# A three-stage kernel (pooled attention, eight-expert MoE, max-of-three FFN): paired k/v transposes, a second products point per iteration, and the first group's columns in six pieces

## The chip, the cores and the metric

One core of one Trainium2 chip runs the whole program. The metric is device microseconds for one launch; lower is better. Engines are named as in the profile: PE (TensorE matmul), PEld (its weight load), DVE (VectorE), ACT (ScalarE), POOL (GpSimd), SP (the queue that issues most DMAs).

## What is computed

Cut to what matters:

```python
# 1. attention, q/k/v [8, 8, 576, 64]; k and v are mean-pooled by 8 along the sequence (576 -> 72)
scores = q @ k_pooled.T / sqrt(64);  attn = softmax(scores);  x = attn @ v_pooled      # -> [4608, 512]
# 2. MoE with 8 experts, top 1 of cosine logits / tau; w1 [8,512,1024], w2 [8,1024,512]
out[token] = gate[token] * (relu(x[token] @ w1[e]) @ w2[e])
# 3. FFN, m1..m3 [512, 768], mo [768, 512]
y = max(x @ m1, x @ m2, x @ m3) @ mo                                                     # [4608, 512]
```

Everything is float32. Matmuls of stages 2 and 3 split each operand into a high and a low float32r part and take three products.

## The kernel before, in words

**Stage 1 (attention, about the first 205 us).** There are 36 tiles of 128 query rows; batches b = 0..7 are taken in pairs, nine tiles a pair, the middle tile being half of one batch and half of the next. A Python loop (line 1441) writes one software-pipelined iteration `it` after the other into the engines' queues: `boundary()`, then `stage_s` of tile it-1 (scores, line 380), `stage_a` of tile it-3 (transposes of the softmaxed scores, line 427), `stage_q` of tile it (transposes of q, line 365), `stage_e` (exp), `stage_x` of tile it-4 (attention times v, line 447), then the jobs that `todo[it]` names. Each engine executes its queue in this order.

Jobs are steps of `prep_steps(b)` (line 248): the pooling of k and v by adding halves three times (`pool_k2`, line 263, and `pool_v`, line 275, both on POOL, for b > 1; `pool_k`, line 255, a DVE reduction, for b = 0 and 1), `dup_k` (line 271, ACT copies pooled k beside itself so that a transpose gives k on both halves of the partitions), `spread_v` (line 280, POOL writes v by head into `vbd`), `trans_k` (line 291: five PE transposes, ACT copies into the block-diagonal `kbd`), `trans_v` (line 303: five more transposes of pooled v and a copy into `vT`), and `vdot` (line 313: ten small matmuls of `vT` with the normalized expert embedding, which give the router's logits in extra columns of `vbd`). k is cut in rows 128, 128, 128, 120, 72 (`KC`) and v in 128 x 4, 64 (`RC`). With `need` the iteration at which batch b is first used, the steps for b > 1 are due at need-7 (-5 for b = 2), need-3 (-2 for b = 2), need-1, need, need, need+1, need+2 (lines 1428 to 1434).

**Routing (inside stage 1 and the start of stage 2).** Chains of small DVE steps (`rank_steps` line 565, `early_steps` line 668, `final_steps`) are dripped in by `fill(n)` between the operations of the iterations (line 875). When a chain yields "pe" it wants the PE: `boundary()` (line 890) turns the state "pe" into "products" at one call, at the next call it runs the step that issues the matmuls (whose state is then "wait"), and at the call after that it lets the chain go on with the results. `boundary()` is called once an iteration. After the first 24 tiles the chain rank_steps(2) + early_steps is queued (at it 27, where `dense[0]` becomes 2); its end, `early_start` (line 924), loads the first expert's weights and issues the gather of the first item's rows (`gather`, line 953, an indirect DMA on POOL into `xrow`).

**Stage 2 (MoE, about 205 to 726 us).** `run` (line 1291) takes 22 items: 18 pairs of 128-row blocks and then singles. An item has eight steps: four weight pieces of w1 (`mm1`) and four of w2 (`mm2`). Each step splits the piece two steps ahead (`split`: ACT casts `whi`, then DVE or POOL subtracts for `wlo`), and `hhi`, `hlo` are ACT and DVE results that the next product needs. `between` (line 1320) is called twice a step. Once the routing is done it advances two generators: `conversions` (cv) and `combinations` (cb), which prepare the weights of stage 3. In the last pair and the singles (from item 17 on, `last_pairs`) `between` advances cb twice instead of once. The end of cb is `columns(0, 1)` (line 1236): it loads the first 768 columns of stage 2's result in four pieces of [128, 2, 2, 192] through one buffer `yr` (two DMAs a piece on SP), waits three yields, and then makes the sums and splits that stage 3 needs (`sums`, line 1260: six DVE and three ACT instructions in five yields).

**Stage 3 (FFN, from 726 us).** `second` (line 1530) takes six groups of 768 rows; the columns of each later group are loaded whole, in two pieces with two buffers, while the group before it finishes.

Of the kernel before, what the change touches and what calls it, by code (L numbers as in the profile page):

```python
# [8 lines left out]
F32 = mybir.dt.float32  # L9
# [5 lines left out]
A = mybir.AluOpType  # L15
# [6 lines left out]
def attention_moe_moe_kernel(  # L22
# [93 lines left out]
    if True:  # L116
# [61 lines left out]
        if True:  # L178
# [69 lines left out]
            def prep_steps(b):  # L248
                kt, vt = kv[b]
                kb, vb = kbds[b % 3], vbds[b % 3]  # L250
                kp = qp.tile([P, 5, 2, D], F32, tag="kp", name=f"kp{b}")
                vp = qp.tile([P, 5, D], F32, tag="vp", name=f"vp{b}")
                vT = qp.tile([D, 5, P], F32, tag="vT", name=f"vT{b}", bufs=1)

                def pool_k(c):
# [5 lines left out]
                        pool_k(c)  # L261

                def pool_k2():
                    for c0, c1, n in ((0, 3, P), (3, 4, KC[3]), (4, 5, KC[4])):
                        for w in (4, 2, 1):
                            dst = kt[0:n, c0:c1, 0:w, :] if w > 1 else kp[0:n, c0:c1, 0:1, :]
                            nc.gpsimd.tensor_tensor(
                                dst, kt[0:n, c0:c1, 0:w, :], kt[0:n, c0:c1, w : 2 * w, :], op=A.add
                            )
# [4 lines left out]

                def pool_v(c0, c1, n):
                    for w in (4, 2, 1):
                        dst = vt[0:n, c0:c1, 0:w, :] if w > 1 else vp[0:n, c0:c1, :].unsqueeze(2)
                        nc.gpsimd.tensor_tensor(dst, vt[0:n, c0:c1, 0:w, :], vt[0:n, c0:c1, w : 2 * w, :], op=A.add)

                def spread_v():  # L280
                    for c, (h0, h1) in enumerate(HS):
# [9 lines left out]
                def trans_k(cs, h0, h1):  # L291
                    ps = pq.tile([P, 512], F32, tag="pq", name=f"ptk{b}_{h0}")
                    col = 0
                    for c in cs:
                        n = KC[c]
                        nc.tensor.transpose(
                            ps[:, col : col + n], kp[0:n, c].rearrange("p two d -> p (two d)"), ident[0:n, 0:n]
                        )
                        col += n
                    nc.scalar.copy(kb[0:D, h0:h1, 0, :], ps[0:D, 0:col].rearrange("p (h s) -> p h s", s=SP))  # L300
                    nc.scalar.copy(kb[D:P, h0:h1, 1, :], ps[D:P, 0:col].rearrange("p (h s) -> p h s", s=SP))

                def trans_v(c0, c1):
                    ps = pq.tile([P, 512], F32, tag="pq", name=f"ptv{b}_{c0}")
# [31 lines left out]
                        lambda: vdot(),  # L336
                    ]
                if b == 1:
                    pk = [lambda: (pool_k(0), pool_k(1)), lambda: (pool_k(2), pool_k(3)), lambda: pool_k(4)]
                    pk += [lambda: (pool_v(0, 4, P), pool_v(4, 5, 64))]  # L340
                else:
                    pk = [lambda: (pool_k2(), pool_v(0, 4, P), pool_v(4, 5, 64))]
                return pk + [
                    lambda: (dup_k(), spread_v()),
                    lambda: trans_k(range(4), 0, 7),
# [832 lines left out]
            def combinations():  # L1178

                for i in range(3):
                    while i not in whole:
                        yield
                    m_ = mraw[i]
                    for p_ in range(F2C // 2):
                        fa, fb = slice(p_ * P, (p_ + 1) * P), slice((3 + p_) * P, (4 + p_) * P)
                        a11, a12, a21, a22 = m_[:, 0:2, fa], m_[:, 2:4, fa], m_[:, 0:2, fb], m_[:, 2:4, fb]  # L1190
                        st = tl["stage"].tile([P, 2, 14, P], F32R, tag="wst", name=f"wst{i}_{p_}")
                        hi, lo = st[:, 0], st[:, 1]
                        sm = tl["stage"].tile([P, 8, P], F32, tag="wsum", name=f"wsum{i}_{p_}")
# [12 lines left out]
                        nc.scalar.copy(hi[:, 6:14, :], sm)  # L1206
                        gt_(lo[:, 4:6, :], a22, hi[:, 4:6, :].bitcast(F32), op=A.subtract)
                        yield
                        gt_(lo[:, 6:14, :], sm, hi[:, 6:14, :].bitcast(F32), op=A.subtract)
                        nc.gpsimd.dma_start(wdram[3 * p_ + i], st.rearrange("p a b f -> p (a b f)").bitcast(F32))  # L1210
                        if p_ == F2C // 2 - 1:
                            combined.append(i)
                        for _ in range(10):
                            yield
                while 3 not in whole:
                    yield
                for f in range(F2C):
# [10 lines left out]
                for _ in columns(0, 1):  # L1228
                    yield

            yhl = []
# [1 line left out]
            def split_o(f):  # L1233
                nc.vector.tensor_tensor(olo[:, f, :], mraw[3][:, f, :], ohi[:, f, :].bitcast(F32), op=A.subtract)

            def columns(g, bufs):

                w_ = HW // 2 if bufs == 1 else HW
                rows = []
                for c in range(2):
                    for n in range(0, HW, w_):
                        t = tl["yr"].tile([P, 2, 2, w_], F32, tag="yr", name=f"yr{g}_{c}_{n}", bufs=bufs)
# [3 lines left out]
                        if bufs == 1:  # L1250
                            for _ in range(3):
                                yield
                            yield from sums(t, c, n, w_)
                        rows.append((t, c, n, w_))
                if bufs > 1:
                    yield
                    for a_ in rows:
                        yield from sums(*a_)

            def sums(t, c, n, w_):  # L1260
                hi, lo = (x_[:, :, n : n + w_] for x_ in yhl[2 * c : 2 * c + 2])
# [58 lines left out]
            def between(half, p_=0):  # L1320

                if not routed:
                    return
                if queue:
                    if half == 0:
                        boundary(p_ in (0, 1, 2, 3, 7))
                    fill(3)
                else:
                    for _ in range(1 + (half and p_ % 2)):
                        next(cv, None)  # L1330
                    next(cb, None)
                    if last_pairs:
                        next(cb, None)

            p0 = prep_steps(0)
            p0[0]()
# [91 lines left out]
            for b in range(1, B):  # L1428
                need = (b // 2) * 9 + (0 if b % 2 == 0 else 4)
                at_ = [need - 7, need - 3, need - 1, need, need, need + 1, need + 2]  # L1430
                at_ = {1: [2, 3, 3, 2, 3, 4, 4, 5, 6, 7], 2: [need - 5, need - 2] + at_[2:]}.get(b, at_)
                for j, t in enumerate(at_):
                    todo.setdefault(t, []).append((b, j))
            qorder = [(m, p_) for m in range(B // 2) for p_ in range(3)]
# [6 lines left out]
            for it in range(NT + 4):  # L1441
# [14 lines left out]
                    load_q(*qorder[qnext])  # L1456
                    qnext += 1
                while kvnext < B and kvnext * 4.5 - 11 <= it:
                    kv[kvnext] = (load_rows("kraw", k, kvnext, KC), load_rows("vraw", v, kvnext, RC))
                    kvnext += 1  # L1460
                if 0 <= it - 1 < NT:
                    stage_s(it - 1)
# [7 lines left out]
                    squares.pop()()  # L1470
                if it >= NT + 2:
                    next(first)
                if 0 <= it - 4 < NT:
                    stage_x(it - 4)
                if it == NT + 1:
# [54 lines left out]
    def second(st, groups, again=False):  # L1530
# [140 lines left out]
        for k_ in range(3):  # L1671
            load_chunk(k_)
        tokens(groups[0])
        ahead = columns(groups[0], 2) if again else iter(())
        for g in groups:
            for _ in ahead:
                pass
            for n in range(CH):
                quad(g, n, groups.index(g) * CH + n)
            nxt = g + 1 in groups  # L1680
            ahead = columns(g + 1, 2) if nxt else iter(())
            next(ahead, None)
            if nxt:
                tokens(g + 1)
# [80 lines left out]
```

## Time and profile before

| what | value |
|---|---|
| median of the runs, lowest, highest | 1281.93 us, 1281.42, 1282.61 |
| the profiled execution's own time | 1281.78 us |
| its span (first to last instruction) | 1279.9 us |
| PE busy | 1225.6 us of the span |

The 1.9 us between the span and the time of the profiled execution lie around the program. A row of a timeline is: start us, duration us, engine, line, operation, tiles written <- read, shape, count, and in brackets how long the engine sat idle just before it and what ended that. A row of the waits is: who waited for whom: us in total, times, the longest. A row of windows is: the stretch, its length, busy us of each engine with the number of instructions, the granted share of the PE's full clock, the mean busy share of the DMA engines, GB/s.

### The profile page before, as it was taken

What the parts mean: (1) busy time and instruction counts of PE and PEld (TensorE: products, weight loads), DVE (VectorE), ACT (ScalarE), POOL (GpSimd) and SP (SyncE); (2) the same over time, 40 slices, a digit from 0 to 9 for tenths busy, and PEclk for the clock granted to TensorE, in tenths of its full rate; (3) what the DMA queues carried; (4) which work ended last, traced back from release to release, by engine and by line L of the source; (5) the groups of instructions that cost most, each with busy time, mean ns of one, the idle gap of its engine ahead of it and who ended that gap; (6) DMA issues with size and microseconds to landing.
All of it is one profiled execution on the core that took longest, in us unless ns stands there. A gap on an engine that the chain in (4) does not pass through costs nothing. (4 is left out here: it accounts for less than half of the span.)

```text
span 1279.9 us, 22372 instructions
## 1 busy us (share of the span) xinstructions
PE 1225.6 (96%) x8281; PEld 1164.2 (91%) x8281; DVE 802.7 (63%) x1551; ACT 581.4 (45%) x1040; POOL 346.5 (27%) x357
## 2 busy tenths in 40 slices
PE   4999998989899999999989999999999999999997
PEld 3888787989899999999979899899998998998995
DVE  6776784788789899899654446355256345345450
ACT  2566555435566666666535423333234223223231
POOL 7985643434500403223000300201302103103101
PEclk9899999999999999999999999999999999999999
DMA  9867335421885644953516768367376475664631
GB/s 261 252 202 214 121 113 206 150 82 35 232 286 199 217 147 161 292 175 132 190 50 229 265 238 304 115 248 280 119 266 231 165 253 209 210 240 181 226 146 52
DMA packets 100088, 246.21 MB, mean 192 GB/s; under 512 B 17102, under 2 KB 57084, under 8 KB 91908
## 3 DMA queue, kind: packets, MB, share of 16 engines
q1 hardware_dynamic: 90660, 201.67, 47.3%
q0 software_dynamic: 9312, 43.04, 9.5%
q8 instruction: 67, 1.10, 0.3%
q14 instruction: 49, 0.40, 0.1%
HBM read 252.23 MB, written 46.98 MB: 234 GB/s over the span
## 5 line engine op out<-in xcount | busy, mean ns | idle before, releaser
L1579 PE MATMUL p<-yhi,wt 128*128 128x384 f32 x1512 | 387.2, 336 | 0.7 <-ACT yo L1093 0.7
L1579 PEld LDWEIGHTS p<-yhi,wt 128*128 128x128 f32 x1512 | 273.5, 188 | 1.4 <-ACT yo L1093 0.9
L1579 PE MATMUL p<-ylo,wt 128*128 128x384 f32 x756 | 254.0, 336 | 0.0
L1587 ACT COPY s<-p 128x384 f32<-128x384 f32 x162 | 77.8, 480 | 222.2 <-PE p L1579 214.0
L1021 PE MATMUL ph<-xhi,whi 128*128 128x256 f32 x576 | 164.9, 286 | 8.0 <-DVE hlo L1037 8.0
L1069 PE MATMUL py<-hhi,wlo 128*128 128x256 f32 x576 | 164.0, 285 | 3.3 <-DVE wlo L1001 3.3
L1069 PE MATMUL py<-hhi,whi 128*128 128x256 f32 x576 | 165.4, 287 | 1.0 <-ACT whi L999 1.0
L1021 PE MATMUL ph<-xhi,wlo 128*128 128x256 f32 x576 | 163.8, 284 | 1.9 <-DVE wlo L1001 1.9
L1021 PE MATMUL ph<-xlo,whi 128*128 128x256 f32 x576 | 163.7, 284 | 1.2 <-DVE xlo L988 1.2
L1069 PE MATMUL py<-hlo,whi 128*128 128x256 f32 x576 | 163.5, 284 | 0.0
L1579 PEld LDWEIGHTS p<-ylo,wt 128*128 128x128 f32 x756 | 142.1, 188 | 0.5
L1608 DVE TENSOR_TENSOR blk<-p,s 128x384 f32<-128x384 f32 x108 | 59.7, 553 | 114.1 <-PE p L1579 113.9
L1564 POOL DMA_INDIRECT gt<-gbuf,ix x26 | 37.1, 1428 | 322.4 <-DMA ix<-idbuf 316.0
L1021 PEld LDWEIGHTS ph<-xhi,whi 128*128 128x128 f32 x576 | 111.0, 193 | 9.6 <-DVE hlo L1037 9.2
L1069 PEld LDWEIGHTS py<-hhi,wlo 128*128 128x128 f32 x576 | 111.0, 193 | 4.1 <-DVE wlo L1001 4.1
L1021 PEld LDWEIGHTS ph<-xhi,wlo 128*128 128x128 f32 x576 | 111.2, 193 | 2.3 <-DVE wlo L1001 2.3
L1021 PEld LDWEIGHTS ph<-xlo,whi 128*128 128x128 f32 x576 | 111.1, 193 | 1.4 <-DVE xlo L988 1.4
L1069 PEld LDWEIGHTS py<-hhi,whi 128*128 128x128 f32 x576 | 111.1, 193 | 1.2 <-ACT whi L999 1.2
L1069 PEld LDWEIGHTS py<-hlo,whi 128*128 128x128 f32 x576 | 111.2, 193 | 0.0
L1001 DVE TENSOR_TENSOR wlo<-w2raw,whi 128x1024 fp32r<-128x1024 f32 x78 | 94.8, 1221 | 9.5 <-ACT whi L999 9.5
L961 POOL DMA_INDIRECT xrow<-xbuf,idg x40 | 69.6, 1740 | 113.4 <-PE px L982 87.8
L999 ACT CAST whi<-w2raw 128x1024 fp32r<-128x1024 f32 x88 | 91.8, 1044 | 5.5 <-PE py L1069 3.9
(307 smaller groups left out, 2338.0 us busy)
## 6 DMA issues: line engine op xcount, KB each, us to landing
wt<-wdram SPq DMA_DIRECT2D x51, 1792.0 KB
w1raw<-in_moe_w_dram SPq DMA_DIRECT2D x88, 512.0 KB
w2raw<-in_moe_w_dram SPq DMA_DIRECT2D x88, 512.0 KB
wdram<-wst POOLq DMA_DIRECT2D x9, 1792.0 KB, 7.2
ybuf<-yo SPq DMA_DIRECT2D x40, 256.0 KB
cvraw<-in_moe_w_dram SPq DMA_DIRECT2D x36, 256.0 KB
vraw<-in_v_dram SPq DMA_DIRECT2D x8, 1024.0 KB
xbuf<-x SPq DMA_DIRECT2D x16, 512.0 KB
```

Of the source, the lines that this page charges most:

```text
L961: nc.gpsimd.indirect_dma_start(out=t[:, j, :], out_offset=None, in_=xbuf[0:nr, :], in_offset=bass.IndirectOffsetOnAxis(ap=idg[:, b_ : b_ + ...
L999: nc.scalar.copy(hi, src)
L1001: eng.tensor_tensor(lo, src, hi.bitcast(F32), op=A.subtract)
L1021: nc.tensor.matmul(ps[:, f, :], a_[:, c, fs], b_[:, c, :], start=(n == 0), stop=(n == 3 * DC - 1))
L1069: nc.tensor.matmul(py[:, c // 2, (c % 2) * 256 : (c % 2 + 1) * 256], a_[:, f, c * P : (c + 1) * P], b_[:, f, :], start=(piece == 0 and f = ...
L1564: nc.gpsimd.indirect_dma_start(out=gt[g][:, j : j + 1], out_offset=None, in_=gbuf[:, :], in_offset=bass.IndirectOffsetOnAxis(ap=cols[j], a ...
L1579: nc.tensor.matmul(ps, a_, b_, start=(start and c + n == 0), stop=(c == 1 and n == 2), skip_group_check=True)
L1587: nc.scalar.copy(t, ps)
L1608: tt(src, add[0], add[1], op=A.add)
```

## The change

Four things.

1. **Side-by-side transposes, b > 1.** Pooled v is written beside pooled k in one tile, both in rows 128 x 4, 64. One set of five transposes gives k on the upper and v on the lower partitions of the same PSUM tile. `dup_k` and `trans_v` go; `trans_kv` copies k to both halves of `kbd` and v to `vT`. There are five steps instead of seven, and `vdot` comes one iteration earlier. `pool_k2` has two groups of rows instead of three. The first addition of `pool_v` is cut in two instructions (for all b). k is loaded by two DMAs instead of three.
2. **b = 1:** the five DVE reductions `pool_k` come at iterations 1, 2, 2, 3, 3 instead of 2, 2, 3, 3, 3.
3. **Products twice an iteration:** while `dense[0]` is 2 and it < 36, `boundary()` is called a second time, ahead of `stage_x`.
4. **Columns of the first group:** six pieces of [128, 2, 2, 128] with two buffers, the first two loaded eight yields ahead, each later one loaded when the piece two before it is done; and cb is no longer advanced twice in the last items. The later groups keep their two whole pieces.

```diff
-                vp = qp.tile([P, 5, D], F32, tag="vp", name=f"vp{b}")
+                vp = kp[:, :, 1, :] if b > 1 else qp.tile([P, 5, D], F32, tag="vp", name=f"vp{b}")
...
-                    for c0, c1, n in ((0, 3, P), (3, 4, KC[3]), (4, 5, KC[4])):
+                    for c0, c1, n in ((0, 4, P), (4, 5, RC[4])):
...
                 def pool_v(c0, c1, n):
                     for w in (4, 2, 1):
-                        dst = vt[0:n, c0:c1, 0:w, :] if w > 1 else vp[0:n, c0:c1, :].unsqueeze(2)
-                        nc.gpsimd.tensor_tensor(dst, vt[0:n, c0:c1, 0:w, :], vt[0:n, c0:c1, w : 2 * w, :], op=A.add)
+                        for a0 in range(c0, c1, 2) if w == 4 else (c0,):
+                            a1 = min(a0 + 2, c1) if w == 4 else c1
...
+                def trans_kv(cs, r0):
+                    ps = pq.tile([P, 512], F32, tag="pq", name=f"ptk{b}_{r0}")
+                    col = 0
+                    for c in cs:
+                        n = RC[c]
+                        nc.tensor.transpose(
+                            ps[:, col : col + n], kp[0:n, c].rearrange("p two d -> p (two d)"), ident[0:n, 0:n]
+                        )
+                        col += n
+                    a0 = 0
+                    while a0 < col:
...
+                        nc.scalar.copy(kb[0:D, at_[0], 0, at_[1]], src)
+                        nc.scalar.copy(kb[D:P, at_[0], 1, at_[1]], src)
+                        a0 = a1
+                    nc.scalar.copy(vT.rearrange("p c r -> p (c r)")[:, r0 : r0 + col], ps[D:P, 0:col])
...
-                    pk = [lambda: (pool_k(0), pool_k(1)), lambda: (pool_k(2), pool_k(3)), lambda: pool_k(4)]
+                    pk = [lambda c=c: pool_k(c) for c in range(5)]
...
-                    pk = [lambda: (pool_k2(), pool_v(0, 4, P), pool_v(4, 5, 64))]
+                    return [
+                        lambda: (pool_k2(), pool_v(0, 4, P), pool_v(4, 5, 64)),
+                        spread_v,
+                        lambda: trans_kv(range(4), 0),
+                        lambda: trans_kv([4], 4 * P),
+                        vdot,
+                    ]
...
-            def columns(g, bufs):
-                w_ = HW // 2 if bufs == 1 else HW
+            def columns(g, whole_=True):
+                w_ = HW if whole_ else HW // 3
...
+                load(0)
+                load(1)
+                for _ in range(1 if whole_ else 8):
                     yield
-                    for a_ in rows:
-                        yield from sums(*a_)
+                for k_ in range(len(at_)):
+                    yield from sums(*rows[k_])
+                    load(k_ + 2)
...
                     next(cb, None)
-                    if last_pairs:
-                        next(cb, None)
...
-                at_ = {1: [2, 3, 3, 2, 3, 4, 4, 5, 6, 7], 2: [need - 5, need - 2] + at_[2:]}.get(b, at_)
+                at_ = {1: [1, 2, 2, 3, 3, 2, 3, 4, 4, 5, 6, 7], 2: [need - 5, need - 2] + at_[2:4] + at_[5:6]}.get(b, at_[:4] + at_[5:6])
...
+                if dense[0] == 2 and it < NT:
+                    boundary()
```

## Rows read from the trace of the kernel before

**Rows 1.** The page: the busy time of each engine over the span.
```profile
PE 1225.6 (96%) x8281; PEld 1164.2 (91%) x8281; DVE 802.7 (63%) x1551; ACT 581.4 (45%) x1040; POOL 346.5 (27%) x357
```

**Rows 2.** Waits of PE in the first 430 us.
```profile
PE psc L401 <- DVE sh L419: 4.9, 2, 2.7
...
PE pav L455 <- DVE dt L480: 2.9, 2, 2.5
```

**Rows 3.** Windows: stage 2, its end, and a stretch of stage 1.
```profile
490.00:610.00 120.00, 120.00 (x1007) 120.00 (x1006) 109.56 (x199) 79.46 (x117) 32.54 (x17) 1.00 0.59 198
610.00:672.00 62.00, 54.88 (x430) 53.11 (x430) 36.18 (x51) 29.50 (x44) 2.00 (x2) 0.97 0.38 123
110.00:120.00 10.00, 10.00 (x78) 9.17 (x77) 7.27 (x20) 7.48 (x22) 9.65 (x15) 1.00 0.59 183
```

**Rows 4.** Timeline of PE around one batch's transposes of v.
```profile
113.12 0.24 PE L307 MATMUL ptv<-ident,vp 64*64 64x64 f32 x1
113.29 1.25 PE L401 MATMUL psc<-kbd,qT 128*128 128x144 f32 x8
...
117.29 0.63 PE L307 MATMUL ptv<-ident,vp 128*64 128x128 f32 x4
117.75 1.15 PE L401 MATMUL psc<-kbd,qT 128*128 128x144 f32 x8
```

**Rows 5.** Timeline of DVE: two points of the early routing chain.
```profile
176.48 0.15 DVE L512 TENSOR_TENSOR cnt<-cnt,prk 128x8 f32<-128x8 f32 x1
...
199.57 0.16 DVE L518 TENSOR_SCALAR idg<-va 128x10 int32<-128x10 f32 x1
```

**Rows 6.** Timeline of PE where stage 2 begins.
```profile
201.01 2.00 PE L455 MATMUL pav<-vbd,aT 128*128 128x146 f32 x12
206.34 0.33 PE L982 MATMUL px<-ident,xrow 128*128 128x128 f32 x1 [3.33 <-DMA xrow<-xbuf,idg]
...
212.02 0.38 PE L1021 MATMUL ph<-xhi,whi 128*128 128x256 f32 x1
```

**Rows 7.** Windows: the same stretch.
```profile
203.00:212.00 9.00, 5.27 (x26) 4.68 (x25) 2.85 (x7) 5.51 (x13) 6.23 (x4) 0.81 0.68 216
```

**Rows 8.** Waits of DVE from 605 to 672 us.
```profile
DVE ysum L1266 <- DMA yr<-ybuf: 10.2, 4, 2.8
```

**Rows 9.** Timeline of ACT: the last copy of items 14 to 17 of stage 2.
```profile
589.48 1.07 ACT L1080 COPY yo<-py 128x512 f32<-128x512 f32 x2 [1.90 <-PE py L1069]
...
613.38 1.07 ACT L1080 COPY yo<-py 128x512 f32<-128x512 f32 x2 [1.95 <-PE py L1069]
...
639.17 1.07 ACT L1080 COPY yo<-py 128x512 f32<-128x512 f32 x2 [1.38 <-PE py L1069]
...
671.59 1.07 ACT L1080 COPY yo<-py 128x512 f32<-128x512 f32 x2 [5.33 <-PE py L1069]
```

**Rows 10.** Timelines of SP, DVE and PE: one column piece and the product behind it.
```profile
640.08 0.89 SPq L1249 DMA_DIRECT2D yr<-ybuf  x2
...
643.34 0.56 DVE L1266 TENSOR_TENSOR ysum<-yr 128x384 f32<-128x384 f32 x1 [2.35 <-DMA yr<-ybuf]
...
648.76 0.39 PE L1021 MATMUL ph<-xhi,whi 128*128 128x256 f32 x1 [3.08 <-DVE hlo L1037]
```

**Rows 11.** Groups on POOL in stage 1, by shape: busy us, mean ns.
```profile
L278 POOL TENSOR_TENSOR vraw<-vraw 128x1024 f32<-128x1024 f32 x8 | 18.9, 2357 | 7.0 <-DMA vraw<-in_v_dram 7.0
...
L267 POOL TENSOR_TENSOR kraw<-kraw 128x768 f32<-128x768 f32 x6 | 10.8, 1808 | 0.0
L278 POOL TENSOR_TENSOR vraw<-vraw 128x512 f32<-128x512 f32 x8 | 10.2, 1272 | 0.6
```

**Rows 12.** Timelines of DVE and POOL near 32 us.
```profile
31.76 4.09 DVE L516 TENSOR_SCALAR thr<-iof 128x36 f32<-128x36 f32 x1
...
32.01 2.05 POOL L284 TENSOR_TENSOR vbd<-vp,mslot 128x128 f32<-128x128 f32 x5
34.02 2.88 POOL L267 TENSOR_TENSOR kraw<-kraw 128x768 f32<-128x768 f32 x2
```

More of the change, by code (lines that the diff above doesn't have):

```diff
@@ L276, in pool_v @@
                     for w in (4, 2, 1):
-                        dst = vt[0:n, c0:c1, 0:w, :] if w > 1 else vp[0:n, c0:c1, :].unsqueeze(2)
-                        nc.gpsimd.tensor_tensor(dst, vt[0:n, c0:c1, 0:w, :], vt[0:n, c0:c1, w : 2 * w, :], op=A.add)
+                        for a0 in range(c0, c1, 2) if w == 4 else (c0,):
+                            a1 = min(a0 + 2, c1) if w == 4 else c1
+                            dst = vt[0:n, a0:a1, 0:w, :] if w > 1 else vp[0:n, a0:a1, :].unsqueeze(2)
+                            nc.gpsimd.tensor_tensor(
+                                dst, vt[0:n, a0:a1, 0:w, :], vt[0:n, a0:a1, w : 2 * w, :], op=A.add
+                            )
                 def spread_v():
@@ L301, in trans_k @@
                     nc.scalar.copy(kb[D:P, h0:h1, 1, :], ps[D:P, 0:col].rearrange("p (h s) -> p h s", s=SP))
+                def trans_kv(cs, r0):
[5 more added lines that the diff above has]
+                            ps[:, col : col + n], kp[0:n, c].rearrange("p two d -> p (two d)"), ident[0:n, 0:n]
+                        )
+                        col += n
+                    a0 = 0
+                    while a0 < col:
+                        h, s_ = divmod(r0 + a0, SP)
+                        if s_ == 0 and col - a0 >= SP:
+                            nh = (col - a0) // SP
+                            a1 = a0 + nh * SP
+                            src, at_ = ps[0:D, a0:a1].rearrange("p (h s) -> p h s", s=SP), (slice(h, h + nh), slice(0, SP))
+                        else:
+                            a1 = min(col, a0 + SP - s_)
+                            src, at_ = ps[0:D, a0:a1], (h, slice(s_, s_ + a1 - a0))
+                        nc.scalar.copy(kb[0:D, at_[0], 0, at_[1]], src)
+                        nc.scalar.copy(kb[D:P, at_[0], 1, at_[1]], src)
+                        a0 = a1
+                    nc.scalar.copy(vT.rearrange("p c r -> p (c r)")[:, r0 : r0 + col], ps[D:P, 0:col])
                 def trans_v(c0, c1):
@@ L1227, in combinations @@
                 tl["yr"] = pool(left, "yrow0", 1, "right")
-                for _ in columns(0, 1):
+                for _ in columns(0, False):
                     yield
@@ L1234, in split_o, with load @@
                 nc.vector.tensor_tensor(olo[:, f, :], mraw[3][:, f, :], ohi[:, f, :].bitcast(F32), op=A.subtract)
-            def columns(g, bufs):
-                w_ = HW // 2 if bufs == 1 else HW
+            def columns(g, whole_=True):
+                w_ = HW if whole_ else HW // 3
+                at_ = [(c, n) for c in range(2) for n in range(0, HW, w_)]
                 rows = []
-                for c in range(2):
-                    for n in range(0, HW, w_):
-                        t = tl["yr"].tile([P, 2, 2, w_], F32, tag="yr", name=f"yr{g}_{c}_{n}", bufs=bufs)
+                def load(k_):
+                    if k_ < len(at_):
+                        c, n = at_[k_]
+                        t = tl["yr"].tile([P, 2, 2, w_], F32, tag="yr", name=f"yr{g}_{c}_{n}", bufs=2)
                         src = ybuf[:, GW * g : GW * g + GW].rearrange("(i c p) (j n) -> c p i j n", i=2, c=2, j=2)
@@ L1249, in columns @@
                             nc.sync.dma_start(t[:, i], src[c, :, i, :, n : n + w_])
[L1250 to L1253, printed above, removed]
                         rows.append((t, c, n, w_))
-                if bufs > 1:
+                load(0)
+                load(1)
+                for _ in range(1 if whole_ else 8):
                     yield
-                    for a_ in rows:
-                        yield from sums(*a_)
+                for k_ in range(len(at_)):
+                    yield from sums(*rows[k_])
+                    load(k_ + 2)
             def sums(t, c, n, w_):
@@ L1458, in attention_moe_moe_kernel @@
                 while kvnext < B and kvnext * 4.5 - 11 <= it:
-                    kv[kvnext] = (load_rows("kraw", k, kvnext, KC), load_rows("vraw", v, kvnext, RC))
+                    kv[kvnext] = (load_rows("kraw", k, kvnext, KC if kvnext < 2 else RC), load_rows("vraw", v, kvnext, RC))
                     kvnext += 1
@@ L1673, in second @@
         tokens(groups[0])
-        ahead = columns(groups[0], 2) if again else iter(())
+        ahead = columns(groups[0]) if again else iter(())
         for g in groups:
@@ L1680, in second @@
             nxt = g + 1 in groups
-            ahead = columns(g + 1, 2) if nxt else iter(())
+            ahead = columns(g + 1) if nxt else iter(())
             next(ahead, None)
```

## The prediction

> **What bounds the kernel now.** I read the page first: PE is busy for 1225.6 of 1279.9 us [rows 1], so a change can gain only by taking work from PE, by filling its 54 us of idle time, or by keeping its clock up. The windows of 10 us over the whole span then show where PE is below 10.00. In stage 2 from 490 to 610 us it is never idle at a granted clock of 1.00, with DVE at 109.56 of 120 us; from 610 to 672 us it is idle for 62 - 54.88 = 7.1 us at a mean clock of 0.97 [rows 3]. Where stage 2 begins it is idle for 3.7 of 9.0 us at a clock of 0.81 [rows 7]. In stage 1 after its first 45 us PE is full but for a few waits on DVE, the longest 2.5 and 2.7 us [rows 2]; a usual stretch has PE at 10.00, ACT at 7.48 and DVE at 7.27 of 10 us [rows 3]. Stage 3 is full of PE work and the change leaves its code as it was. So each part below is weighed by what it does to PE.
>
> **Transposes of v.** In the timeline of PE the start of each instruction follows the one before it closely, so its cost is the distance of the starts. For one batch the 64-row transpose takes 113.29 - 113.12 = 0.17 us and the four others 117.75 - 117.29 = 0.46 us [rows 4]; no PE wait stands between. The six batches b > 1 lose these five transposes each: 6 x 0.63 = **3.8 us** of PE, in a stretch where PE is the bound. The transposes of k stay five (64 rows in place of 72, 128 in place of 120). ACT's copies become eight a batch in place of nine (three of `dup_k`, four of k, two of v, against four of k, two slivers of eight columns and two of v), more of them in one iteration; ACT stands at 7.48 of 10 us [rows 3] and PE needs `kbd` an iteration later, so I cost that at nothing; without that cover it would be an ACT copy or two ahead of a score product. `vdot` one iteration earlier waits for nothing new: it moves with the v transposes. POOL's pooling must now be done by need-1 for v too; the POOL timeline has each batch pooled two iterations or more ahead of that. SP issues one DMA less a batch. Nothing queues behind these.
>
> **Products twice an iteration.** The routing chain takes from its first products' results at 176.48 to its last result `idg` at 199.57 us [rows 5], over four iterations of some 4.9 us with a wait of three `boundary()` calls in them. Written out by the calls, each of the two products is consumed one iteration earlier: the second results come two iterations, or some 9.7 us, earlier. With them go the loads of the first expert's w1 on SP and the gather on POOL. PE now stands from 203.01 (201.01 + 2.00) to 206.34 us for the gathered rows, 3.33 us [rows 6]. That wait goes even if only one iteration is won (4.9 > 3.33). The stretch 203 to 212 us also has a granted clock of 0.81, that is, part of it at 1.2 GHz: 0.19 x 9 = 1.7 us, and 9.00 - 5.27 = 3.7 us idle [rows 7]. Sum **5.4 us**. Next after the gather would be `wlo` of the first piece, which POOL makes behind ACT's cast; the weights come earlier by the same step and the cast with them. The second call's matmuls are the same ones, put before `stage_x`; PE would wait there only if POOL's slot rows were late, and those are ready an iteration ahead. Bounds: nothing (if the gather's place is taken by the weights) to 5.4; I take 5.4 since every instruction on the way moves.
>
> **Columns of the first group.** With one buffer a piece is loaded only after the piece before it is done, and used three yields later: the load issued at 640.08 us lands at 643.34, and DVE and ACT, which run in order, stand still for it [rows 10]. DVE lost 10.2 us in four such waits [rows 8]; PE's largest gap there, 3.08 us, is a wait for `hlo`, which stood behind them [rows 10]. Priced twice: by the windows, 7.1 us idle and 0.03 x 62 = 1.9 us of clock, 9.0 us [rows 3]; by the items, 671.59 - 613.38 = 58.2 us for two items where the one before them took 613.38 - 589.48 = 23.9, so 10.4 us [rows 9]. With two buffers a load is out for five yields, two and a half steps of 3 us, 7.5 us against a landing after 3.3. What is added: twelve more DVE instructions in all (six pieces of six for four), at most 12 x 0.56 = 6.7 us by the 128 x 384 one [rows 10], spread over two items in which DVE has 62 - 36.18 = 26 us free [rows 3]. I take **9.0 us**; the lower end is 4, if the hand-offs between ACT and DVE inside `sums` were behind half of it, the upper 10.4. The later groups run the same instructions in the same order: nothing.
>
> **POOL's additions and b = 1.** Small DVE operations on SBUF stall while POOL works: `thr`, 128 x 36, took 4.09 us and ended only when POOL had passed five instructions of `vbd` and the first addition of `kraw` [rows 12]. The change makes that first addition of k longer (four row groups in place of three: 2.36 in place of 1.81 us, by the same shape of v) and cuts v's 2.36 us in two of 1.27, 2.54 together [rows 11]. Since DVE did not get in between the five independent instructions of `vbd`, I expect it not to get in between two halves either. That gives longer stalls by 0.2 to 0.55 us where one falls on PE's path, three times at most as now: +0.2 to +1.6. The DVE reduction moved to it 1 falls where DVE idles for the first scores, and takes 1 us from in front of b = 1's `kbd`: -1.0 to 0. Together I take +0.4, bounds -1.5 and +1.6.
> The Trainium skill (SBUF — State Buffer, "Who interferes with whom") says the pair of ports that DVE and GpSimd share is locked for one whole instruction, and that whoever issues first holds it. By that a cut instruction would let DVE in half-way; the five instructions that `thr` sat through here speak against it.
>
> **Sum.** 1281.8 (the profiled execution; the median of the runs is 0.15 us above it) - 3.8 - 5.4 - 9.0 + 0.4 = **1264.0 us**.
>
> **Rivals.**
> - *The column stage keeps half its loss.* If DVE and ACT waiting for each other, not the load, is what PE feels, 4 to 5 us are won in place of 9. For it: with conversions the same kind of hand-off runs at full PE, which speaks against. 1268.5.
> - *The earlier chain does not reach the gather.* A step that ends in "pe" an iteration later than I count, or POOL slot rows that come late, leaves the wait at 203 us: 1264.0 + 5.4 = 1269.4. Against it is the margin of two iterations.
> - *DVE gets in between the halves.* Each stall that meets v's first addition is then shorter by 1.1 us, on the three PE waits of this kind up to 3.3 us [rows 2, 11]: 1261. For it speaks only that these are separate instructions.
> - *Slower: POOL's longer first addition catches DVE in more places.* The place is the routing steps of stage 1, dripped between operations on which PE waits. One hit costs PE up to 2.5 us [rows 2] and, if the clock falls as at 203 us, 1.7 us more [rows 7], so 4.2. One new hit for each of the six batches would be 25 us: 1264.0 + 25.2 = 1289. It decides from five new hits (21 us against 18 won). For it: POOL is at 9.65 of 10 us beside the pooling [rows 3]; against it: its total work falls, and today only three of the many overlaps cost PE anything.
>
> **How the numbers follow.** The forecast as summed, within 3 us, has 0.60; half the columns 0.15; the gather unmoved 0.06; DVE let in 0.10; slower 0.03; and 0.06 for two of the misses at once, about 1273, or for a gain that is nearly all given back. About 0.2%, 2.6 us, is what a measurement of this kernel can tell from no change. All cases but the slower one and a piece of the last lie far below that bound: faster 0.95, same 0.02, slower 0.03. The range takes in the forecast's bounds (9.0 to 10.4 in the columns, -1.5 in the last term: 1260.7), DVE let in, half the columns and the gather unmoved: 1259.5 to 1270.5; what is left out is 1273 and above and a thin lower edge.
>
> **What would show it.** Right: no `ptv` rows, and five transposes a batch less on PE; `idg` near 190 us and no PE wait for `xrow`; the clock at 1.00 near 205 us; no wait of DVE or ACT on `yr` between 600 and 672 us, and items 16 and 17 of stage 2 at 24 us each. Wrong: gaps of PE behind `hlo` in those items though the loads are in; DVE operations of 4 us or more in stage 1 in more places than now, with PE idle behind `sh` or `dt`; a granted clock below 1.00 in new stretches of stage 1.

## The result, and the profile after

The changed kernel takes 1268.39 us (median of 4 runs, 1264.20 to 1270.12) against 1282.27 us (4 runs, 1281.42 to 1282.78). The ratio is 0.9887, with a 95% interval of [0.9869, 0.9906]: faster by 12.1 to 16.8 us. The forecast was 1264.0 us, within 1259.5 to 1270.5. The profiled execution took 1268.24 us, 13.5 us less than the one before, with a span of 1266.5 us. In the page PE has 8281 - 8251 = 30 instructions less, the five transposes of six batches:

```profile
PE 1223.4 (97%) x8251; PEld 1165.0 (92%) x8251; DVE 805.8 (64%) x1563; ACT 579.8 (46%) x1040; POOL 344.7 (27%) x347
```

**Where the time went.** Six stretches and the items 6 to 15, which take 239.0 us in every run and are left out, add up to the whole span. Their bounds are starts in the timelines: `pqT` of tile 9 and of tile 35 on PE, and the last `yo` copy of items 0, 5, 15 and 17 of stage 2 on ACT. In us, one profiled execution each; the kernels further down are the experiments of the next section (the last one is the ninth).

| kernel | to tile 9 | tiles 9 to 35 | to item 0 | items 1 to 5 | items 16, 17 | rest | span |
|---|---|---|---|---|---|---|---|
| before | 63.68 | 131.61 | 46.14 | 132.95 | 58.21 | 608.31 | 1279.9 |
| after | 58.98 | 136.88 | 40.55 | 134.91 | 47.37 | 608.81 | 1266.5 |
| after, again | 62.49 | 133.89 | 40.56 | 132.48 | 47.37 | 608.21 | 1264.0 |
| columns alone | 60.22 | 132.53 | 45.92 | 130.63 | 47.37 | 608.23 | 1263.9 |
| twice alone | 63.21 | 133.01 | 40.56 | 131.61 | 59.12 | 607.49 | 1274.0 |
| copies, after | 60.00 | 125.99 | 40.60 | 134.14 | 47.37 | 607.50 | 1254.6 |

Two stretches fall about as forecast: 5.6 us to item 0 and 10.8 us in items 16 and 17. The stretch of tiles 9 to 35, in which all 30 transposes of v of the six batches lie and which should give 3.8 us, is 5.3 us longer. The first stretch gave 4.7 us that nobody forecast, and items 1 to 5 took 2.0 us more, around a wait for a weight transfer (`cvraw`) that the change does not touch (PE's clock from 320 to 330 us was 0.76 this time, below).

The last copies of items 14 to 17 on ACT (timeline of the changed kernel) against [rows 9]: 23.9 us from the second to the third, 23.5 to the last, where 25.8 and 32.4 were.

```profile
586.42 1.07 ACT L1115 COPY yo<-py 128x512 f32<-128x512 f32 x2 [1.91 <-PE py L1104]
...
610.32 1.07 ACT L1115 COPY yo<-py 128x512 f32<-128x512 f32 x2 [1.95 <-PE py L1104]
...
634.22 1.07 ACT L1115 COPY yo<-py 128x512 f32<-128x512 f32 x2 [1.40 <-PE py L1104]
...
657.69 1.07 ACT L1115 COPY yo<-py 128x512 f32<-128x512 f32 x2 [4.75 <-PE py L1104]
```

Windows of PE in the changed kernel (start:end, length, busy us and instructions, granted clock, DMA share, GB/s). The last row answers to [rows 3] and the sixth to [rows 7]: both stretches are full now, at a clock of 1.00. The first five lie in the part of stage 1 that got worse.

```profile
70.00:150.00 80.00, 72.48 (x492) 0.89 0.55 173
80.00:90.00 10.00, 7.04 (x47) 0.82 0.18 63
90.00:100.00 10.00, 9.81 (x63) 0.84 0.74 207
130.00:140.00 10.00, 6.85 (x32) 0.71 0.10 35
140.00:150.00 10.00, 10.00 (x61) 0.78 0.13 54
190.00:210.00 20.00, 20.00 (x147) 1.00 0.64 211
320.00:330.00 10.00, 6.64 (x43) 0.76 0.86 287
610.00:658.00 48.00, 48.00 (x404) 1.00 0.48 146
```

The same windows of the kernel before:

```profile
70.00:150.00 80.00, 74.68 (x558) 0.98 0.60 182
80.00:90.00 10.00, 9.41 (x76) 1.00 0.74 236
90.00:100.00 10.00, 8.32 (x55) 0.83 0.48 145
130.00:140.00 10.00, 6.95 (x55) 1.00 0.43 148
140.00:150.00 10.00, 10.00 (x78) 1.00 0.14 54
```

From 70 to 150 us PE is idle 2.2 us longer, and the granted clock is 0.89 in place of 0.98, which on 80 us is about 7 us of speed. A window between 0.50 and 1.00 mixes 1.2 and 2.4 GHz. What PE waited for is in the timelines of DVE, POOL and PE of the changed kernel:

```profile
76.80 4.14 DVE L551 TENSOR_SCALAR lg<-lg,rtau 128x72 f32<-128x72 f32 x1
...
84.39 2.75 DVE L617 COPY pre<-oh 128x72 f32<-128x72 f32 x1
...
129.62 3.91 DVE L547 TENSOR_TENSOR oh<-w,wm 128x72 f32<-128x72 f32 x1
...
76.54 2.04 POOL L288 TENSOR_TENSOR vbd<-kp,mslot 128x128 f32<-128x128 f32 x5
78.54 3.69 POOL L267 TENSOR_TENSOR kraw<-kraw 128x1024 f32<-128x1024 f32 x2
...
84.59 3.82 POOL L280 TENSOR_TENSOR vraw<-vraw 128x512 f32<-128x512 f32 x3
...
129.11 2.04 POOL L288 TENSOR_TENSOR vbd<-kp,mslot 128x128 f32<-128x128 f32 x5
131.11 3.67 POOL L267 TENSOR_TENSOR kraw<-kraw 128x1024 f32<-128x1024 f32 x2
...
81.75 1.49 PE L422 MATMUL psc<-kbd,qT 128*64 128x144 f32 x16 [2.79 <-DVE mxl L559]
...
90.19 2.26 PE L436 MATMUL psc<-kbd,qT 128*128 128x144 f32 x8 [1.40 <-DVE pre L547]
...
133.82 3.55 PE L490 MATMUL pav<-vbd,aT 128*128 128x146 f32 x12 [3.15 <-DVE dt L515]
```

The ends are what to read. `lg` ends at 76.80 + 4.14 = 80.94. POOL's five `vbd` and the first addition of `kraw` (2.347 us by its shape) end at 78.54 + 2.35 = 80.89. `oh` ends at 133.53, that addition at 131.11 + 2.35 = 133.46. `pre` ends at 87.14, the second half of the cut `vraw` addition at 84.59 + 2 x 1.27 = 87.13. Each time DVE comes free when POOL reaches the first instruction that reads what the one before it wrote: the addition of quarters behind that of halves. Independent instructions on POOL in a row act on DVE as one. `thr` in [rows 12] ended in the same way, at 35.85 against 34.02 + 1.81. It is the rule over all fourteen profiles: 43 steps of DVE that are not reductions took over 2 us in the first 205 us, and each ended 0.01 to 0.28 us behind the end of such a sequence of independent instructions.

### The profile page after: what moved, and what is told of

Read it like the earlier page. It is cut to its first block, busy times and chain, and to the rows that moved or that the text cites. A ratio compares the mean times of both kernels' runs of the same rounds, so it can differ in the third digit from the quotient of the medians.

```text
span 1266.5 us, 22316 instructions
## 1 busy us (share of the span) xinstructions
PE 1223.4 (97%) x8251; PEld 1165.0 (92%) x8251; DVE 805.8 (64%) x1563; ACT 579.8 (46%) x1040; POOL 344.7 (27%) x347
```

## The experiments

Twelve kernels ran. Comparisons below are of medians with the kernel before on the same chip.

**1. The columns alone.** Part 4 of the change (the new `columns`, its calls, and no second `next(cb)` in the last items), on the kernel before.

> The kernel before with the columns part alone (six pieces, two buffers, eight yields ahead). Theory (the load that waits for its buffer is the whole loss): items 16 and 17 of stage 2 take some 47.4 us together in place of 58.2, and the time falls by 10 to 11 us, to about 1271.5. Rival (the part sets off something else in stage 1, or the pieces only gain beside the earlier start): the items keep part of the loss and the time falls by 4 to 6 us, to about 1277.

1269.42 us against 1283.21, ratio 0.9906 [0.9870, 0.9942]. Items 16 and 17 take 47.37 us to the hundredth, as in every run with this part. So the whole loss went with the waits for these loads. Which of the four things in this part did it (the smaller pieces, the second buffer, the lead of eight yields, the slower pace of cb) no run separates. The runs with one buffer took 58.2 to 62.6 us here, depending on the execution, so the 10.8 us between the two first profiles is the low end of what this part gives.

**2. Products twice an iteration, alone.**

```diff
+                if dense[0] == 2 and it < NT:
+                    boundary()
                 if 0 <= it - 4 < NT:
                     stage_x(it - 4)
```

> The kernel before with the second boundary call an iteration alone. Theory: idg comes some 9.7 us earlier, PE does not wait for xrow, and the stretch from pqT of tile 35 to the end of item 0 is 5 to 6 us shorter; the time falls by 5 to 6 us, to about 1276.5. Rival (the chain is earlier only because stage 1 around it has changed): the wait for xrow stays, the time is the same within 1 us.

1275.43 us, ratio 0.9938 [0.9913, 0.9963]. The stretch to item 0 takes 40.56 in place of 46.14 us: 5.6 us, the same as in the changed kernel. PE goes from the product before it to the gathered rows without a wait, where [rows 6] had 3.33 us. In the timelines of this kernel the first row is DVE's, the others PE's:

```profile
189.72 0.16 DVE L518 TENSOR_SCALAR idg<-va 128x10 int32<-128x10 f32 x1
...
201.94 2.00 PE L455 MATMUL pav<-vbd,aT 128*128 128x146 f32 x12
203.87 1.09 PE L982 MATMUL px<-ident,xrow 128*128 128x128 f32 x8
```

**3. The transposes alone.** `trans_kv`, `pool_k2` with two groups of rows, k loaded in two pieces, the shorter list of steps and its due times, on the kernel before; v's first addition uncut, b = 1 as before.

> The kernel before with the side-by-side transposes and k's longer first addition on POOL, v's first addition uncut, b = 1 as before. Theory (the longer runs of additions on POOL hold DVE's routing steps and cost PE what the transposes give): 3.8 us off for the transposes, up to 9 back for DVE steps of 4 us near 77 and 130 us and the half clock behind them, so the time is between 1278 and 1287, and tile 35's pqT comes no earlier than before. Rival (the additions cost nothing, the loss of the changed kernel's stage 1 came from b = 1's order or from the cut): 1278, pqT of tile 35 at 191.5.

1284.68 us, ratio 1.0008 [0.9986, 1.0031]: 30 PE instructions less and no gain. Of the two places that I named, the one near 77 us did not come; at the other `oh` took 3.91 us at 133.90 and PE waited 2.99 us for `dt` behind it. Tiles 9 to 35 took 131.3 us, as before, and the way to tile 9 was 4.5 us longer, which is more than I expected from this part.

**4. b = 1's additions alone.**

```diff
-                    pk = [lambda: (pool_k(0), pool_k(1)), lambda: (pool_k(2), pool_k(3)), lambda: pool_k(4)]
+                    pk = [lambda c=c: pool_k(c) for c in range(5)]
...
-                at_ = {1: [2, 3, 3, 2, 3, 4, 4, 5, 6, 7], 2: [need - 5, need - 2] + at_[2:]}.get(b, at_)
+                at_ = {1: [1, 2, 2, 3, 3, 2, 3, 4, 4, 5, 6, 7], 2: [need - 5, need - 2] + at_[2:]}.get(b, at_)
```

> The kernel before with b = 1's additions of k one row group an iteration, and nothing else. Theory (the 4.7 us that the changed kernel has won by 45 us come from rows of v that land late enough for DVE's first steps to slip through ahead of POOL, not from this part): thr still takes 4 us, tile 9's pqT comes within 1 us of before, and the time is the same within 1 us. Rival (this part wins them): tile 9's pqT comes 3 to 5 us earlier and the time falls by up to 4.7 us, unless a later wait takes it back.

1280.13 us, ratio 0.9981 [0.9959, 1.0004]: not told from no change. My theory's details missed: `thr` took 1.28 us, not 4 (`thq` behind it took 3.46), and tile 9 came 2.1 us earlier than before. But runs whose code is that of the kernel before as far as tile 9 got there at 60.2 and 63.2 us too (experiments 1 and 2). What this part gives is smaller than what the start differs by from run to run. Alone, the four parts add up to 1.7%, uncertain by some 0.5; the changed kernel gave 1.1%, and 1.3% when it ran again (below).

**5. v's first addition in one piece again.** The changed kernel without the cut in `pool_v`. **6. Later routing.** The changed kernel with the first two routing chains queued three iterations later:

```diff
-                    if it - 4 == t1 - 1 and t1 < NT1:
+                    if t1 < NT1:
+                        if it - 4 == t1 + 2:
+                            queue.append([chain(rank_steps(m), slot_steps(nc.gpsimd))])
+                        continue
+                    if it - 4 == t1 - 1 and t1 < NT1:
                         queue.append([chain(rank_steps(m), slot_steps(nc.gpsimd))])
```

**7. The changed kernel again**, on the same chip as these two.

> The changed kernel with v's first addition on POOL in one piece again. Theory (DVE does not get in between two halves, which stand back to back on POOL): the time is the same within 1 us of the changed kernel, or up to 1 us shorter, since two halves take 2.54 us in place of 2.36. By the rule of the Trainium skill (SBUF - State Buffer, Who interferes with whom), the pair of ports is given free after each instruction: then the uncut addition makes the DVE steps that meet it 1.1 us longer, and the time rises by 1 to 3 us.

> The changed kernel with the first two routing chains queued three iterations later, so that their DVE steps near 77 and 130 us fall behind POOL's additions instead of beside them. Theory (the loss of stage 1 is DVE steps held by POOL and the half clock behind the PE wait): no DVE step over 3 us at 70 to 145 us, no PE wait behind lg or oh there, the granted clock at 1.00 or nearly so, pqT of tile 35 at 188 to 192 in place of 195.9, the time 4 to 8 us below the changed kernel, about 1260 to 1264. Rival (the chains' own steps cost PE, wherever they stand): the waits come back 15 us later and the time is the same within 1 us.

> The changed kernel once more, for its spread. Theory (the early lead depends on when the rows of v land against POOL's start): its runs spread over some 4 us or more, and where the profile has thr at 4 us the early lead of 4.7 us is gone. Rival (the spread is chance on the chip as with any kernel): runs within 1 us of 1268.4 and the same early lead.

Uncut: 1265.44 us, 0.9865 [0.9847, 0.9883]. Again: 1266.66 us, 0.9871 [0.9853, 0.9889]. The cut makes no difference to the time, and none to the hold, as the timelines of DVE show. In the uncut kernel one addition of 2.36 us stands on POOL, in the changed kernel again two of 1.27 us. The uncut one:

```profile
82.90 2.61 DVE L613 COPY pre<-oh 128x72 f32<-128x72 f32 x1
```

The changed kernel again:

```profile
84.72 2.75 DVE L617 COPY pre<-oh 128x72 f32<-128x72 f32 x1
```

So the hold is not given up between two instructions. The Trainium skill (SBUF — State Buffer, "Who interferes with whom") gives the kind of step that can be held, a copy, a `tensor_scalar` or one with two inputs in SBUF, and the rows agree: `lg`, `oh` and `pre` are of that kind, and the reductions beside them (`mx`, 0.75 us at 88.43 in the changed kernel) keep their length. That the hold lasts for one instruction of the other engine is not what these rows show.

Run again, the changed kernel lay within 1.7 us, so it does not spread by 4 us on every chip. Its early lead was 1.2 us, not 4.7. Not `thr` but `thq`, the step behind it, was held this time, for 4.44 us; my theory put the spread on `thr` alone, which was too narrow. A hold alone does not tell the two executions apart either: in the first `im` was held for 4.12 us at 33.98. The granted clock does: from 20 to 60 us it was 1.00 in the first and 0.83 in this one.

Later routing: 1262.37 us, 0.9830 [0.9808, 0.9852], 4.3 us below the changed kernel again. The first collision is gone and tiles 9 to 35 take 128.86 us, 5.0 less. The second was only moved, onto another batch's additions at 138 us, where it is worse. The timelines of DVE, POOL and PE:

```profile
137.77 3.38 DVE L547 TENSOR_TENSOR lg<-lg,mxl 128x72 f32<-128x72 f32 x1
...
138.72 3.67 POOL L267 TENSOR_TENSOR kraw<-kraw 128x1024 f32<-128x1024 f32 x2
...
144.24 6.21 PE L490 MATMUL pav<-vbd,aT 128*64 128x146 f32 x24 [4.44 <-DVE dt L515]
```

And its windows of PE: from 70 to 150 us the clock is 1.00 but for this one place.

```profile
70.00:150.00 80.00, 75.16 (x553) 0.96 0.60 188
140.00:150.00 10.00, 5.76 (x22) 0.66 0.14 55
```

**8. A copy of one element behind `vbd`.** If DVE is let in where a POOL instruction depends on the one before it, a tiny instruction that reads the last result must let it in. `brk` is a new tile of one column.

```diff
                             mslot[0:n, SL[c] : SL[c + 1], :].to_broadcast(sh),
                             op=A.mult,
                         )
+                    nc.gpsimd.tensor_copy(brk[0:1, :], vb[0:1, SL[4], 0:1])
```

**9. Such copies everywhere.** k's first addition is cut in two as v's is, with a copy behind each first half. **10. The same, with the first routing chain three iterations later.**

```diff
+                        for a0 in range(c0, c1, 2) if w == 4 else (c0,):
...
+                            if a1 < c1:
+                                nc.gpsimd.tensor_copy(brk[0:1, :], kt[0:1, a0, 0, 0:1])
```

> The changed kernel with one copy of a single element on POOL behind the five instructions of vbd of each batch, reading what the fifth of them wrote. Theory (a routing step of DVE that meets POOL's independent instructions is held until POOL comes to one that depends on the one before it): where lg, oh or thq took 3.9 to 4.4 us they are let go behind vbd or held only by what follows, so none is over 2.6 us, the PE waits of 2.8 to 3.2 us behind them fall to 1 us or less, and the time falls by 2 to 5 us from the changed kernel, to about 1263. Rival (DVE waits for POOL's bytes, however they are cut, or for a real pause): the steps take as long as before and the time is the same within 1 us, or a little longer for the copies.

> The same, and both first additions of each batch (k's as well as v's) cut in two with such a copy between the halves. Theory: a hold lasts at most about one half, 1.3 us, or vbd, 2.0 us; no DVE step at 70 to 150 us over 2.1 us, PE waits there under 1 us, the clock at 1.00, tile 35's pqT at 187 to 191, the time 5 to 8 us below the changed kernel, about 1260. Rival: POOL's longer work (some 0.2 us a copy, 0.2 us a cut) only delays it; the same within 1 us or up to 2 us slower.

> The same with the first routing chain queued three iterations later as well. Theory: nothing is left at 77 us for the later chain to win, so within 1.5 us of the run with all copies; if the copies do not let DVE in, it wins what the first collision costs, 2 to 4 us against the changed kernel.

Against 1282.50 us: 1262.55 us (0.9843 [0.9822, 0.9864]), 1256.83 us (0.9795 [0.9779, 0.9811]) and **1254.98 us (0.9786 [0.9767, 0.9805])**. All three are below the changed kernel on this scale (0.9871 and 0.9887), the second and third by the whole of their intervals; these two are not told apart, though their medians lie 1.85 us apart where I expected 1.5 at most. In the first, the timelines of DVE and POOL show the hold end just ahead of the copy and a new one begin behind it:

```profile
129.66 1.37 DVE L549 TENSOR_TENSOR oh<-w,wm 128x72 f32<-128x72 f32 x1
...
131.38 2.44 DVE L549 TENSOR_TENSOR pre<-pre 128x72 f32<-128x72 f32 x1
...
129.14 2.04 POOL L289 TENSOR_TENSOR vbd<-kp,mslot 128x128 f32<-128x128 f32 x5
131.25 0.17 POOL L295 COPY brk<-vbd 1x1 f32<-1x1 f32 x1
131.38 3.68 POOL L268 TENSOR_TENSOR kraw<-kraw 128x1024 f32<-128x1024 f32 x2
```

`oh` meets the same five instructions as before and ends at 131.03, just ahead of the copy, in place of staying through the addition (1.37 us for 3.91). That is 0.15 us before the last of `vbd` ends, so it is hardly the copy's own work that lets DVE in; the copy keeps the next addition from following at once. An idle POOL does the same: in the changed kernel again `tokid`, a conversion, starts at 22.22 beside five `vbd` that end at 24.11, and is done at 23.90; POOL has nothing to do behind them until 26.70. `pre` is then held by the uncut addition alone: 131.38 + 2.35 = 133.73, and it ends at 133.82. One step, `pre` at 84.83, took 2.78 us through v's two halves, where no copy stands, so my bound of 2.6 us for all steps was too low. PE's wait behind `oh` fell to 0.85 us, below the 1 us that I expected, but other waits are longer than that: 2.23 us at 84.52, 2.10 at 89.76 and 1.53 at 135.97.

With all copies no step of DVE takes over 2.1 us from 70 to 150 us, and PE's clock stays at 1.00. Waits of 1.45 and 1.06 us are left, above the 1 us I expected. Windows of PE:

```profile
70.00:150.00 80.00, 76.03 (x573) 1.00 0.59 186
80.00:90.00 10.00, 8.51 (x71) 1.00 0.37 129
120.00:130.00 10.00, 8.36 (x69) 1.00 0.71 239
130.00:140.00 10.00, 9.17 (x69) 1.00 0.13 52
```

The changed kernel again:

```profile
70.00:150.00 80.00, 74.04 (x517) 0.91 0.58 181
```

Tiles 9 to 35 take 125.99 us, 7.9 less than in the changed kernel again: from 70 to 150 us PE is idle 2.0 us less (76.03 against 74.04 us busy), and the clock of 1.00 in place of 0.91 gives about 0.09 x 80 = 7 us more.

**11. The copies on the kernel before, with nothing of the change. 12. The same with the transposes.**

> The kernel before with the one-element copies on POOL behind vbd and between the halves of the first additions, and nothing of the change. Theory (the holds of DVE are an old loss that the change only made larger): the two hits at 88 and 132 us shrink, the stretch from tile 9's pqT to tile 35's takes 127 to 129 us in place of 131.6, the time falls by 3 to 5 us, to about 1278. Rival (only the changed kernel's longer runs cost PE): the same within 1 us.

> The same with the side-by-side transposes, which makes it the run with the transposes alone and the copies. Theory (the transposes are worth what their rows on PE say once nothing is held): from tile 9's pqT to tile 35's 3 to 4 us less than in the run without them, about 124.5, and the time less by as much. Rival (the transposes are hidden behind another limit, such as ACT's copies of kbd): the stretch is within 1 us of that of the run without them.

Against 1280.18 us: 1273.34 us (0.9946 [0.9926, 0.9965]) and 1274.97 us (0.9958 [0.9935, 0.9981]). So the holds were an old loss of some 7 us (4.5 to 9.5). The profiles show longer holds and a lower clock with the change; the times alone do not show that the loss grew: the copies gave 0.54% here and 0.76% on the changed kernel, uncertain by 0.2 each. Against the profile of before, 3.3 us lie in tiles 9 to 35 and 5.6 ahead of tile 9, where two kernels with the code of before differ by 3 us (experiments 1 and 2). Tiles 9 to 35 take 128.32 and 127.05 us, 1.3 us apart, not 3 to 4. From `pqT` of tile 9 to that of tile 18, a stretch with the transposes of two batches, the two take 44.48 and 45.25 us; without the waits of PE in it (1.03 and 3.03 us by the timelines) that is 43.45 and 42.22, or 0.62 us less for each batch, just what the rows of the transposes say. But the waits are longer with the transposes. The view of PE's waits from 70 to 150 us in the eleventh kernel:

```profile
PE pav L467 <- DVE dt L492: 1.9, 2, 1.5
PE psc L413 <- DVE sh L431: 1.2, 2, 0.6
```

The same view of the twelfth:

```profile
PE pav L498 <- DVE dt L523: 2.7, 3, 1.5
PE pav L498 <- DVE pre L625: 1.4, 1, 1.4
PE psc L444 <- DVE sh L462: 1.0, 2, 0.6
PE psc L430 <- ACT qT L420: 0.4, 2, 0.2
```

3.1 us against 5.5: PE waits 2.4 us more, in a stretch from which the transposes of three batches, 1.9 us, are gone. Of the 3.8 us, 1.3 are left over tiles 9 to 35, and the time of the kernel does not tell the two apart. Neither theory holds whole; the transposes are worth their rows on PE, and part of that is given back to DVE's steps.

## Why the prediction was right, and where not

- **Transposes, -3.8.** The size was right as work of PE: 0.62 us a batch measured, 0.63 forecast. As time it was not, since the longer runs of independent instructions that come with it on POOL hold DVE longer (below). ACT's copies, costed at nothing, brought small waits: two of 0.2 us for `qT` in the twelfth kernel, and in the changed kernel one of 0.19 us for `qT` at 128 us and one of 0.38 us for `kbd` at 181 us.
- **Products twice an iteration, -5.4.** Right: 5.6 us alone and in the changed kernel. `idg` is ready at 190.42 us in the changed kernel (near 190 was said), PE does not wait for `xrow`, and the clock is 1.00 from 190 to 210 us. The rival in which the chain does not reach the gather fell.
- **Columns, -9.0.** The mechanism was right and the price low: 10.8 us against the profile of before, 47.37 us for the two items in every run with this part. It took the whole loss, the upper end of 10.4 and a little more: items 16 and 17 take 23.9 and 23.5 us. Nothing waits for a load of `yr`. The hand-offs between ACT and DVE, which made half the loss in a rival, cost nothing that shows.
- **POOL's additions and b = 1, +0.4 with bounds -1.5 and +1.6.** This is the step that failed. For tiles 9 to 35 the forecast was 131.61, less six batches of 0.63, plus 0.4: 128.2 us. They took 136.9 and 133.9 us in the two executions, so the term was +9.0 and +6.1 there, and the early lead (4.7 and 1.2 us, not forecast) gave part of it back. I had the mechanism, and even that DVE does not get in between the halves. I priced it by the additional length of an addition, 0.2 to 0.55 us a stall, as if PE's clock stayed where it was. The clock is what most of it was: in the 70 to 150 us its loss rose by about 7 us and the idle time by 2.2, in the second execution by about 5 and 0.6.
- **The rivals on POOL.** That DVE is let in between the halves fell with the uncut run. The slower rival had that price, 4.2 us a hit with the clock, but wanted new hits. In the first profiled execution there was one (`lg` at 76.80), in the second none. The others were at the old places. That of `pre` cost no more clock than before (0.84 and 0.83 from 90 to 100 us); that of `oh` took it down to 0.71 and 0.78 from 130 to 150 us, where in the kernel before this wait left it at 1.00:

```profile
136.28 2.10 PE L455 MATMUL pav<-vbd,aT 128*128 128x146 f32 x12 [2.47 <-DVE dt L480]
```

That profile is the best case, though: in experiments 1, 2 and 4, whose code in these tiles is that of the kernel before, the same wait of 2.44 us went with a clock of 0.91 over these 20 us, and tiles 9 to 35 took 132.5 to 133.0 us. So some 1 us of the term belongs to the profile that I started from.
- **The total.** The profiled execution's span fell by 13.4 us in place of 17.8. The difference of 4.4 us is 8.6 (that term in tiles 9 to 35), 2.0 (items 1 to 5) and 0.5 (the rest), less 1.8 (columns), 0.2 (to item 0) and 4.7 (the early lead). That it stayed in the range is in part luck: no part of the sum stands for the early lead, which was 1.2 us when the kernel ran again (it took 1266.7 us then, since tiles 9 to 35 lost 3 us less). And the median, 1268.4 us, is what the rival with half the columns gave (1268.5), though that rival's mechanism fell.

## What to carry to other kernels

Where small steps of DVE on SBUF stand between PE's operations, look at which instructions POOL has in a row that do not depend on each other: they hold DVE as one, and cutting them changes nothing unless something dependent stands between. Copies of one element there cost 0.17 us each on POOL, and with the first additions cut around them were together worth some 10 us on the changed kernel, most of it clock. Price a wait of PE with the clock that it may take down, from the longest such stretch in the trace, not with the idle time alone.

## What was not expected of the hardware

- **The hold of DVE runs to POOL's first dependent instruction.** Six independent ones (4.14 us), two halves (2.75 us) and one whole addition (2.61 us) each held to their end; with a dependent copy of 0.17 us DVE got in (1.37 us). POOL's own rows differ in the same way: one that is independent of the one ahead starts some 0.04 us before that one has ended (78.54 against 76.54 + 2.04), a dependent one some 0.07 us after (the copy at 131.25 against 129.14 + 2.04). Why that gap lets DVE in, the traces do not show, and no run put a copy there that depends on nothing.
- **The start is a race.** If the rows of v land early, POOL starts on them before DVE has finished normalizing the expert embedding, and DVE's steps are held. The timelines of POOL and DVE in the kernel before:

```profile
14.93 3.69 POOL L278 TENSOR_TENSOR vraw<-vraw 128x1024 f32<-128x1024 f32 x2 [4.16 <-DMA vraw<-in_v_dram]
...
15.10 2.19 DVE L170 TENSOR_TENSOR ent<-eny,ensg 8x1 f32<-8x1 f32 x1
```

And after:

```profile
16.47 2.49 POOL L280 TENSOR_TENSOR vraw<-vraw 128x512 f32<-128x512 f32 x2 [5.72 <-DMA vraw<-in_v_dram]
...
15.36 0.15 DVE L170 TENSOR_TENSOR ent<-eny,ensg 8x1 f32<-8x1 f32 x1
```

In the nine profiles of kernels without the copies, those where POOL started at 15.40 us or later have 5.0 us between `pqT` of tile 0 and of tile 1, those where it started at 14.95 or earlier 7.1 to 7.8 us. So where the transfer lands later, these two tiles are 2 to 3 us closer, whatever the code. It need not last: the second experiment, with 5.0 us, reached tile 9 at 63.2 us, the first, with 7.1, at 60.2. The kernel before ran between 1276.5 and 1291.8 us in these comparisons; how much of that is this race was not tried.
- **One wait of nearly the same length, two clocks.** The stall in item 4 was 3.1 us at a clock of 1.00 before and 3.4 us at 0.76 after, in stretches whose code is the same. The wait for `dt` behind `oh` was 2.47 us at 1.00 before and 2.44 us at 0.91 in experiments 1, 2 and 4. What decides it the runs do not show.
